# SwiGLU feed-forward on one core: the first 256 rows of x loaded two rows to a partition

## The chip, the core and the metric

The kernel runs on one core of a Trainium2 chip. The metric is device time in microseconds (us) of one execution. The core has a matrix engine (PE, TensorE, with its weight loader shown apart as PEld), VectorE (DVE), ScalarE (ACT), GpSimd (POOL) and SyncE (SP). Transfers between the chip's large memory and the on-chip memory are issued by SP and ACT, each on its own queue; a transfer that has been issued runs beside the engines, on 16 DMA engines. The on-chip memory has 128 partitions. PE writes into PSUM, a second small memory, from which DVE or ACT copy.

## The reference

```python
B, S, D, F = 1, 2048, 640, 1536

def reference(x, w_gate, w_up, w_down):
    g = _silu(x @ w_gate)
    u = x @ w_up
    return (g * u) @ w_down
```

All arrays are bf16. x is 2048 x 640, the gate and up weights 640 x 1536, the down weights 1536 x 640.

## The kernel before

PE contracts over partitions. For the two projections the contraction runs over D = 640, five slices of 128 (`kd`), so x is needed transposed: `xT` has D on the partitions and the 2048 rows along the free dimension. The rows are worked in four blocks of 512. In each block, for each of the 12 slices of F (`fc`), PE makes the gate product `pg` and the up product `pu` (lines 192 to 202, five matmuls each), ACT applies silu, DVE multiplies (lines 211 to 217), and the result goes into `aT`. After the twelve slices the block's down product follows (lines 256 to 308), its results are copied out of PSUM by ACT and stored. DVE also works, beside that, on the last four rows by dot products (line 147).

The transposed x comes in two ways. Rows 256 to 2047 are transposed by the DMA (`turn_x`, line 105, issued by SP). Rows 0 to 255 are needed first, and are loaded as they lie and transposed by PE:

- `load_x` (line 86) brings 128 rows per call into `x_sb`, one row of 640 elements (1280 bytes) to a partition. Rows 0 to 127 are loaded on SP's queue, rows 128 to 255 on ACT's; they are the first instructions of both queues.
- Behind them on SP's queue come, in this order, four of the five early gate-weight pieces (line 115; the piece for `kd` 1 is on ACT's queue), the DMA transpose of rows 256 to 511, the first up-weights in two transfers (line 83), and the rest of the weights.
- `head` first runs 18 matmuls on ones (`warm`, line 176), which need no loaded data. Then `transpose_chunk` (lines 180 to 190) transposes the two chunks of 128 rows. For each chunk there are five transposes, one for each slice of D: the 128 x 128 piece of `x_sb` is loaded as PE's weights and the identity streams through. Slices 0 and 1 go into one PSUM tile and are copied by ACT into `xT`, slices 2 to 4 go into another and are copied by DVE (line 190).
- Then the first projections follow in a fixed order (`steps`, lines 230 to 235): for four slices of F at once, slice `kd` 0 on rows 0 to 127, `kd` 0 on rows 128 to 255, then `kd` 1 to 4 on rows 0 to 255, and then all five on rows 256 to 511. After them come the four up products.

The order of PE's and ACT's instructions in the head is kept as written (`keep_order`); every other wait is one for data or for a free buffer. An SP transfer that uses a semaphore again waits for the earlier transfer on it.

Of the kernel before, what the change touches and what calls it, by code (L numbers as in the profile page):

```python
# [10 lines left out]
def _body(  # L11
# [8 lines left out]
    nc = tc.nc  # L20
    P = nc.NUM_PARTITIONS
    f32 = mybir.dt.float32
    bf16 = mybir.dt.bfloat16
# [3 lines left out]
    B, S0, D = x.shape  # L27
    F = w_gate.shape[1]
    S = B * S0
    x2 = x.rearrange("b s d -> (b s) d")  # L30
# [7 lines left out]
    HALF = S_BLK // 2  # L38
# [10 lines left out]
    consts = ctx.enter_context(tc.tile_pool(name="consts", bufs=1))  # L49
    work = ctx.enter_context(tc.tile_pool(name="work", bufs=3))  # L50
    outp = ctx.enter_context(tc.tile_pool(name="outp", bufs=3))
    psum = ctx.enter_context(
        tc.tile_pool(name="psum", bufs=2, space=bass.MemoryType.PSUM)
    )

    ident = consts.tile([P, P], bf16)
    x_sb = consts.tile([P, HALF // P, D], bf16)
    xT = consts.tile([P, KD, S], bf16)
    wg_sb = consts.tile([P, KD, F], bf16)
    wu_sb = consts.tile([P, KD, F], bf16)  # L60
# [9 lines left out]

    make_identity(nc, ident[:])

    x_v = x2.rearrange("(c p) d -> p c d", p=P)
    xt_v = x2.rearrange("s (kd p) -> s kd p", p=P)
    wg_v = w_gate.rearrange("(kd p) f -> p kd f", p=P)
    wu_v = w_up.rearrange("(kd p) f -> p kd f", p=P)
# [2 lines left out]
    def wslice(a, b):  # L79
        return slice(a * P, b * P)  # L80
# [1 line left out]
    def load_w(eng, dst, src, a, b):  # L82
        eng.dma_start(out=dst[:, :, wslice(a, b)], in_=src[:, :, wslice(a, b)])

    def load_x(eng, c0, c1):
        eng.dma_start(out=x_sb[:, c0:c1, :], in_=x_v[:, c0:c1, :])  # L86

    def issue_order(a, b):
        tc.add_manual_dep(
# [18 lines left out]
    silu_first = consts.tile([P, 1], f32)  # L108
    nc.vector.memset(ones[:], 1.0)  # L109

    load_x(nc.sync, 0, 1)
    load_x(nc.scalar, 1, 2)
    for kd in range(KD):
        eng = nc.scalar if kd == 1 else nc.sync
        eng.dma_start(
            out=wg_sb[:, kd, wslice(0, EARLY)], in_=wg_v[:, kd, wslice(0, EARLY)]
# [12 lines left out]
    def turn_w(dst, src, f0, f1):  # L129
# [7 lines left out]
        out=x_row[:],  # L137
        in_=x2[S - T : S, :].rearrange("t d -> (t d)").partition_broadcast(P),
# [40 lines left out]

    def transpose_chunk(c, parts):  # L180
        c_sl = slice(c * P, (c + 1) * P)
        for copy, tag, k0, k1 in parts:
            pt = psum.tile([P, k1 - k0, P], bf16, tag=tag, name="pt")
            for kd in range(k0, k1):
                nc.tensor.transpose(  # L185
                    out=pt[:, kd - k0, :],
                    in_=x_sb[:, c, kd * P : (kd + 1) * P],
                    identity=ident[:],
                )
            copy(out=xT[:, k0:k1, c_sl], in_=pt[:])  # L190

    def proj_step(ps, w_sb, fc, sb, c0, c1, kd):
        nc.tensor.matmul(  # L193
# [25 lines left out]
    def head():  # L219
        dve, act = nc.vector.tensor_copy, nc.scalar.copy  # L220
        split = [(act, "po_a", 0, 2), (dve, "po_b", 2, KD)]
        pgs = [
            psum.tile([P, S_BLK], f32, tag="gu", name="pg", bufs=4)
            for _ in range(EARLY)
        ]
        warm(N_WARM)
        for c in range(HALF // P):
            transpose_chunk(c, split)

        steps = [(0, 0, P), (0, P, HALF)]  # L230
        steps += [(kd, 0, HALF) for kd in range(1, KD)]
        steps += [(kd, HALF, S_BLK) for kd in range(KD)]
        for kd, c0, c1 in steps:
            for fc in range(EARLY):
                proj_step(pgs[fc], wg_sb, fc, 0, c0, c1, kd)

        for fc in range(EARLY):
            pu = psum.tile([P, S_BLK], f32, tag=("po_a", "po_b")[fc % 2], name="pu")
            proj(pu, wu_sb, fc, 0, 0, S_BLK)
            gate(pgs[fc], pu, 0, fc, S_BLK)  # L240
        keep_order(mybir.EngineType.PE)
        keep_order(mybir.EngineType.Activation)

    head()
    for sb in range(NSB):
# [27 lines left out]
        for q in range(P // Q):  # L273
            nc.scalar.dma_start(
                out=out2[
                    sb * S_BLK : sb * S_BLK + n_t, DA + q * Q : DA + (q + 1) * Q
                ].rearrange("(i r) c -> r i c", r=Q),
                in_=ot_q[q * Q : (q + 1) * Q, :].rearrange("r (i c) -> r i c", c=Q),
            )

        for j in range(SUB):
# [6 lines left out]
            for c0, c1, tag in cols:  # L288
# [14 lines left out]
                eng = nc.sync if c1 < D else nc.scalar  # L303
# [82 lines left out]
def kernel(tc, *args):  # L386
    _body(tc, *args)
    tc.close()
    tc.compile()
    _trim(tc.nc)  # L390
# [30 lines left out]
```

## Time and profile before

| | |
|---|---|
| median of three runs | 163.31 us (163.09 to 163.35) |
| profiled execution, first to last instruction (span) | 161.8 us |
| profiled execution, total | not among the answers; the median stands 1.5 us above the span |
| PE busy | 159.4 us (99%), 808 matmuls |
| PEld busy | 77.6 us (48%), 808 weight loads |
| DVE busy | 111.0 us (69%) |
| ACT busy | 42.6 us (26%) |
| DMA | 15.86 MB, mean 98 GB/s |
| ten transposes of x on PE | from 2.31 us, 1.25 us |
| first projection on PE | 3.71 us |

The profile shows one execution. Its times are microseconds from the first instruction. A row of the timeline gives start, length, engine, line of the kernel, operation, what it writes and reads, and a count; in brackets stands the idle time of that engine before it and what ended it. SPq and ACTq are the two queues' issuing instructions; their length is the issue alone. A row of the DMA view gives the time from issue to landing as its last number. A row of the table by stretches gives the stretch, its length, the busy time and count of PE, PEld, DVE, ACT and POOL, the granted clock, the share of the DMA engines and GB/s; with one line of the kernel asked for, only the engines that this line uses. Matmuls overlap, and the length shown of one (0.31 us for 128 columns) is longer than the distance from one to the next.

### The profile page before, as it was taken

To read this page: it belongs to the slowest core of one execution; us is meant where nothing else is said; L and a number is where in the kernel's file an instruction comes from. 1 tells how busy PE (TensorE), PEld (TensorE's weight loads), DVE (VectorE), ACT (ScalarE), POOL (GpSimd) and SP (SyncE) were. 2 spreads that over 40 slices of the span, in tenths; PEclk is the share of its full clock that TensorE was granted. 3 is DMA by queue.
4 is the path that set the end of the run, shared out by engine and by line. 5 is a ranking of instruction groups with operands and counts; after the bars stand their busy time and mean duration, and the time that the engine had idled before them with its cause. 6 is when DMAs were issued, how large, how long until landed. Compare 5 with 4: busy or idle time off the path is not lost.

```text
span 161.8 us, 2142 instructions
## 1 busy us (share of the span) xinstructions
PE 159.4 (99%) x808; PEld 77.6 (48%) x808; DVE 111.0 (69%) x250; ACT 42.6 (26%) x74; POOL 0.6 (0%) x6
## 2 busy tenths in 40 slices
PE   8999999999999999999999999999999999999995
PEld 7854444444444444444444444444444444445454
DVE  2034223599569999989919999979964999993001
ACT  5051222112222222211222322221214222222121
POOL 1000000000000000000000000000000000000000
PEclk9999999999999999999999999999999999999999
DMA  6999999934189999003110000000321000000312
GB/s 212 231 351 349 361 248 231 222 75 91 34 192 159 235 236 184 4 0 34 65 65 0 0 4 2 0 0 3 62 67 34 0 0 0 0 0 4 48 41 73
DMA packets 41961, 15.86 MB, mean 98 GB/s; under 512 B 33504, under 2 KB 41824, under 8 KB 41952
## 3 DMA queue, kind: packets, MB, share of 16 engines
q1 hardware_dynamic: 33584, 14.93, 37.0%
q10 hardware_dynamic: 8368, 0.80, 3.5%
q8 instruction: 6, 0.10, 0.3%
q14 instruction: 3, 0.02, 0.1%
HBM read 6.88 MB, written 2.62 MB: 59 GB/s over the span
## 4 chain that ended last, share of the span: by engine, by line
PE 97%; DMA 2%; SPq 0%; DVE 0%; issue 0%
PE pg L193 32%; PE pu L193 32%; PE po_a L291 26%; PE po_t L261 6%; DMA wg_sb<-in_w_gate_dram 2%; SPq L86 0%; DVE ot_b L302 0%
## 5 line engine op out<-in xcount | busy, mean ns | idle before, releaser
L193 PE MATMUL pg<-xT,wg_sb 128*128 128x512 bf16 (+3 forms) x264 | 59.8, 363 | 0.1
L193 PE MATMUL pu<-xT,wu_sb 128*128 128x512 bf16 (+1 forms) x240 | 59.1, 379 | 0.0
L215 DVE TENSOR_TENSOR aT<-sg,pu 128x512 bf16<-128x512 f32 (+1 forms) x48 | 32.7, 682 | 32.3 <-PE pu L193 32.3
L214 ACT ACTIVATE sg<-pg 128x512 f32<-128x512 f32 (+1 forms) x48 | 28.4, 597 | 71.2 <-PE pg L193 67.4
L291 PE MATMUL po_a<-wd_sb,aT 128*128 128x512 bf16 (+4 forms) x228 | 42.8, 348 | 0.0
L147 DVE SCALAR_TENSOR_TENSOR prod<-wgT,x_row 128x640 f32<-128x640 bf16 x48 | 39.4, 821 | 1.5 <-DMA wgT<-in_w_gate_dram 0.4
L147 DVE SCALAR_TENSOR_TENSOR prod<-wuT,x_row 128x640 f32<-128x640 bf16 x48 | 39.4, 821 | 1.0
L193 PEld LDWEIGHTS <-wg_sb 128*128 128x128 bf16 x264 | 25.9, 100 | 26.8 <-DMA wg_sb<-in_w_gate_dram 0.4
L193 PEld LDWEIGHTS <-wu_sb 128*128 128x128 bf16 x240 | 23.4, 98 | 28.1 <-DMA wu_sb<-in_w_up_dram 0.3
L291 PEld LDWEIGHTS <-aT 128*128 128x128 bf16 x228 | 20.8, 98 | 21.7
L300 ACT CAST ot<-po_a 128x512 bf16<-128x512 f32 (+2 forms) x17 | 9.5, 559 | 31.8 <-PE po_a L291 20.2
L261 PE MATMUL po_t<-aT,wd_sb 128*128 128x512 bf16 (+1 forms) x48 | 10.4, 366 | 0.0
L261 PEld LDWEIGHTS <-wd_sb 128*128 128x128 bf16 x48 | 4.7, 98 | 5.1
L302 DVE CAST ot_b<-po_a 128x96 bf16<-128x96 f32 (+1 forms) x2 | 0.5, 240 | 9.7 <-PE po_a L291 9.6
L270 ACT CAST ot_t<-po_t 128x512 bf16<-128x512 f32 (+1 forms) x4 | 2.2, 559 | 11.6 <-PE po_t L261 11.6
L147 DVE DVE_READ_ACCUMULATOR prod<-wgT,x_row 128x1 f32 x48 | 3.9, 82 | 0.0
L147 DVE DVE_READ_ACCUMULATOR prod<-wuT,x_row 128x1 f32 x48 | 3.9, 82 | 0.0
L272 DVE STREAM_TRANSPOSE ot_q<-ot_t 128x512 bf16<-128x512 bf16 (+1 forms) x4 | 2.7, 676 | 1.7 <-ACT ot_t L270 1.7
L190 DVE COPY xT<-pt 128x384 bf16<-128x384 bf16 x2 | 0.7, 358 | 2.9 <-PE pt L185 2.9
L176 PE MATMUL pw<-ones 128*128 128x128 bf16 x18 | 2.1, 313 | 0.4 <-DVE ones L109 0.4
L176 PEld LDWEIGHTS <-ones 128*128 128x128 bf16 x18 | 1.8, 147 | 0.4 <-DVE ones L109 0.4
L119 ACT ACT_TABLE_LOAD x1 | 1.3, 1283 | 1.0 <-issue 1.0
(13 smaller groups left out, 4.7 us busy)
## 6 DMA issues: line engine op xcount, KB each, us to landing
wd_sb<-in_w_down_dram SPq DMA_DIRECT2D x1, 1920.0 KB, 13.0
out_dram<-ot SPq DMA_DIRECT2D x15, 128.0 KB, 1.7
wg_sb<-in_w_gate_dram SPq DMA_DIRECT2D x2, 640.0 KB, 7.9
wu_sb<-in_w_up_dram SPq DMA_DIRECT2D x2, 640.0 KB, 8.6
wu_sb<-in_w_up_dram SPq DMA_DIRECT2D x2, 320.0 KB, 4.7
x_row<-in_x_dram SPq DMA_DIRECT2D x1, 640.0 KB, 5.1
wg_sb<-in_w_gate_dram SPq DMA_DIRECT2D x4, 128.0 KB, 3.4
out_dram<-ot_q ACTq DMA_DIRECT2D x12, 32.0 KB, 1.9
```

What stands on the lines that cost most here:

```text
L119: nc.scalar.activation(silu_first[:], ones[:, 0:1], ACT.Silu)
L147: nc.vector.scalar_tensor_tensor(out=prod[:], in0=wT[:, fc, :], scalar=1.0, in1=x_row[:, t, :], op0=ALU.mult, op1=ALU.mult, accum_out=acc[ ...
L176: nc.tensor.matmul(pw[:, 0:P], lhsT=ones[:], rhs=ones[:], start=True, stop=True)
L190: copy(out=xT[:, k0:k1, c_sl], in_=pt[:])
L193: nc.tensor.matmul(ps[:, c0:c1], lhsT=w_sb[:, kd, fc * P : (fc + 1) * P], rhs=xT[:, kd, sb * S_BLK + c0 : sb * S_BLK + c1], start=(kd == 0 ...
L214: nc.scalar.activation(sg[:, 0:n_s], pg[:, 0:n_s], ACT.Silu)
L215: nc.vector.tensor_tensor(out=aT[:, fc, s0 : s0 + n_s], in0=sg[:, 0:n_s], in1=pu[:, 0:n_s], op=ALU.mult)
L261: nc.tensor.matmul(po_t[:], lhsT=wd_sb[:, kf, DA:D], rhs=aT[:, kf, sb * S_BLK : sb * S_BLK + n_t], start=(kf == 0), stop=(kf == KF - 1),)
L270: nc.scalar.copy(ot_t[:], po_t[:])
L272: nc.vector.transpose(out=ot_q[:], in_=ot_t[:])
L291: nc.tensor.matmul(po[:], lhsT=aT[:, kf, s0 : s0 + P], rhs=wd_sb[:, kf, c0:c1], start=(kf == 0), stop=(kf == KF - 1),)
L300: nc.scalar.copy(ot[:], po[:])
```

## The change

Rows 0 to 255 are laid out two to a partition: partition p holds rows 2p and 2p + 1, one behind the other, 2560 bytes that are contiguous in the source. The first load brings rows 0 to 127 into partitions 0 to 63 and the second rows 128 to 255 into partitions 64 to 127, on the same two queues as before. A chunk of 128 rows is then 64 partitions, and each of its five slices is transposed in two steps, one for the even rows and one for the odd rows: the weights are 64 rows by 128 columns, and a 64 x 64 part of the identity streams through. That makes twenty transposes in place of ten. In PSUM the even rows of a slice lie ahead of the odd rows; the copies into `xT` write every second column, so that `xT` is as before. Nothing else is changed.

```diff
-    x_sb = consts.tile([P, HALF // P, D], bf16)
+    H = P // 2
+    x_sb = consts.tile([P, 2, D], bf16)
...
-    x_v = x2.rearrange("(c p) d -> p c d", p=P)
+    x_v = x2[0:HALF, :].rearrange("(p r) d -> p r d", r=2)
...
-    def load_x(eng, c0, c1):
-        eng.dma_start(out=x_sb[:, c0:c1, :], in_=x_v[:, c0:c1, :])
+    def load_x(eng, c):
+        eng.dma_start(out=x_sb[c * H : (c + 1) * H], in_=x_v[c * H : (c + 1) * H])
...
-    load_x(nc.sync, 0, 1)
-    load_x(nc.scalar, 1, 2)
+    load_x(nc.sync, 0)
+    load_x(nc.scalar, 1)
...
     def transpose_chunk(c, parts):
         c_sl = slice(c * P, (c + 1) * P)
+        rows = slice(c * H, (c + 1) * H)
         for copy, tag, k0, k1 in parts:
-            pt = psum.tile([P, k1 - k0, P], bf16, tag=tag, name="pt")
+            pt = psum.tile([P, k1 - k0, 2, H], bf16, tag=tag, name="pt")
             for kd in range(k0, k1):
-                nc.tensor.transpose(
-                    out=pt[:, kd - k0, :],
-                    in_=x_sb[:, c, kd * P : (kd + 1) * P],
-                    identity=ident[:],
-                )
-            copy(out=xT[:, k0:k1, c_sl], in_=pt[:])
+                for r in range(2):
+                    nc.tensor.transpose(
+                        out=pt[:, kd - k0, r, :],
+                        in_=x_sb[rows, r, kd * P : (kd + 1) * P],
+                        identity=ident[rows, rows],
+                    )
+            copy(
+                out=xT[:, k0:k1, c_sl].rearrange("d k (p r) -> d k r p", r=2),
+                in_=pt[:],
+            )
```

## The prediction

> **What bounds the kernel now.** I read the page first: busy times, then the chain that ended last.
>
> ```profile
> span 161.8 us, 2142 instructions
> PE 159.4 (99%) x808; PEld 77.6 (48%) x808; DVE 111.0 (69%) x250; ACT 42.6 (26%) x74; POOL 0.6 (0%) x6
> ...
> PE 97%; DMA 2%; SPq 0%; DVE 0%; issue 0%
> PE pg L193 32%; PE pu L193 32%; PE po_a L291 26%; PE po_t L261 6%; DMA wg_sb<-in_w_gate_dram 2%; SPq L86 0%; DVE ot_b L302 0%
> ```
>
> TensorE (PE) is on the chain for 97% of the span. The only other entry of size is one transfer, a piece of the gate weights, 2% of 161.8 = 3.2 us. The change touches only the first microseconds, so I asked for the chain of the first 16 us and then for the timeline there.
>
> ```profile
> 0.45 3.21 DMA wg_sb<-in_w_gate_dram
> 3.66 0.05 issue
> 3.71 5.21 PE pg L193 x44
> 8.92 4.37 PE pu L193 x20
> ```
>
> ```profile
> 0.00 0.39 SPq L86 DMA_DIRECT2D x_sb<-in_x_dram  x1
> 0.13 0.38 ACTq L86 DMA_DIRECT2D x_sb<-in_x_dram  x1
> ...
> 0.45 1.84 SPq L115 DMA_DIRECT2D wg_sb<-in_w_gate_dram  x4
> ...
> 2.31 0.98 PEld L185 LDWEIGHTS <-x_sb 128*128 128x128 bf16 x10
> 2.31 1.25 PE L185 MATMUL pt<-ident,x_sb 128*128 128x128 bf16 x10
> ...
> 2.33 1.91 SPq L105 DMA_TRANSPOSE xT<-in_x_dram  x1
> 2.74 0.37 ACT L190 COPY xT<-pt 128x256 bf16<-128x256 bf16 x1 [0.22 <-PE pt L185]
> 3.06 0.36 DVE L190 COPY xT<-pt 128x384 bf16<-128x384 bf16 x1 [2.73 <-PE pt L185]
> 3.28 0.37 ACT L190 COPY xT<-pt 128x256 bf16<-128x256 bf16 x1 [0.16 <-PE pt L185]
> 3.60 0.36 DVE L190 COPY xT<-pt 128x384 bf16<-128x384 bf16 x1 [0.17 <-PE pt L185]
> 3.71 4.93 PEld L193 LDWEIGHTS <-wg_sb 128*128 128x128 bf16 x44 [0.41 <-DMA wg_sb<-in_w_gate_dram]
> ...
> 4.29 1.15 SPq L83 DMA_DIRECT2D wu_sb<-in_w_up_dram  x2
> ...
> 8.79 4.00 PEld L193 LDWEIGHTS <-wu_sb 128*128 128x128 bf16 x20 [0.15 <-DMA wu_sb<-in_w_up_dram]
> ```
>
> Read it as a race. The path that the change edits (load x, transpose, copy) has its last weight load done at 2.31 + 0.98 = 3.29, and then the weight loader sits 0.41 us until the first gate-weight piece has landed at 3.66. So the edited path is not the one that releases the projections: it has about 0.3 us to spare (0.41 less one step of 0.10). Behind that stand two more waits, which show as breaks between groups of weight loads, and the landing times of the transfers:
>
> ```profile
> 4.96 1.52 PEld L193 LDWEIGHTS <-wg_sb 128*128 128x128 bf16 x14
> ...
> 6.58 2.06 PEld L193 LDWEIGHTS <-wg_sb 128*128 128x128 bf16 x19
> ```
>
> ```profile
> wu_sb<-in_w_up_dram SPq DMA_DIRECT2D x2, 320.0 KB, 4.7
> ...
> x_sb<-in_x_dram SPq DMA_DIRECT2D x1, 160.0 KB, 2.3
> x_sb<-in_x_dram ACTq DMA_DIRECT2D x1, 160.0 KB, 2.6
> ...
> xT<-in_x_dram SPq DMA_TRANSPOSE x1, 4.2
> ```
>
> From 4.96 a 256-column step takes (1.52 - 0.10)/13 = 0.109 us (0.10 is one load's own length, below). Fourteen of them end at 4.96 + 14 x 0.109 = 6.49, but the next starts at 6.58: 0.09 us lost. There the DMA transpose of rows 256-511 lands (2.33 + 4.2 = 6.53). From 6.58, twenty steps end at 8.76 and the up-weights start at 8.79: 0.03 us lost to their landing. After that PE is dense to the end. So the end time is set, in the last place, by SP's queue: those two transfers are issued at 2.33 and 4.29.
>
> **Pace.** The lengths of single instructions in the edited part and in the projections, and PE's work from 3.71 to 4.96 (the columns after the loads' are granted clock, transfer share and GB/s):
>
> ```profile
> L185 PEld LDWEIGHTS <-x_sb x10: 103/151/151, 2.3 to 3.1; 128*128 128x128 bf16 x10
> L185 PE MATMUL pt<-ident,x_sb x10: 288/314/314, 2.3 to 3.2; 128*128 128x128 bf16 x10
> ```
>
> ```profile
> L193 PEld LDWEIGHTS <-wg_sb x44: 95/98/152, 3.7 to 8.5; 128*128 128x128 bf16 x44
> ```
>
> ```profile
> 3.71:4.96 1.25, 1.25 (x10) 1.13 (x11) 1.00 1.01 264
> ```
>
> A transpose of 128 columns takes (1.25 - 0.31)/9 = 0.104 us. From 3.71 eight projection steps of 128 columns and two of 256, 1536 columns, take 1.25 us: 0.81 ns a column. After 4.96 it is 0.109 us for 256: 0.43. So PE works at half pace until about 4.95, although the clock column reads 1.00 there. A delay of PE before 4.95 therefore costs half of itself, and 0.12 us (0.09 + 0.03) are swallowed by the two later waits.
>
> **The change, part by part.**
>
> *Transposes.* Ten 128-row steps go, twenty 64-row steps with 64 moving columns come, each with its own weight load. No 64-row step is in the trace. The nearest row is the last output tile, 64 columns with a weight load each, at full pace:
>
> ```profile
> 159.46 0.46 PE L291 MATMUL po_a<-wd_sb,aT 128*128 128x64 bf16 x10
> ```
>
> ```profile
> L291 PE MATMUL po_a<-wd_sb,aT 128*128 128x64 bf16 x12 | 0.5, 193 | 0.0
> ```
>
> (0.46 - 0.19)/9 = 0.030 us a step; at half pace 0.06. Twenty take 1.2 us where ten take 1.04: 0.16 us more, inside the 0.3 us to spare. Below, it cannot go under 20 x 0.03 = 0.6 us; above, one step can cost as much as a 128-row step (0.104), or a weight load that does not overlap its matmul (0.15, the load's length in these microseconds, + 0.06 = 0.21). I take 0.06, because the 64-column row keeps its weight loads hidden. At 0.104 the projections start at 2.31 + 20 x 0.104 = 4.39, 0.68 late, worth 0.34 at half pace, less 0.12: +0.22 us. At 0.21 they start at 6.5, when 1.24 us of half-pace work (0.62) and 1.52 us of full-pace work stand undone: 2.14 - 0.12 = +2.0 us.
>
> The Trainium skill, "TensorE: Matmul & The Clock Gate", Part 3, "The mechanism", says that a weight load overlaps a running matmul only when it goes to another row group; here all ten steps of a half go to the same one. By that the step would be the 0.21 us above. The trace of the full-height steps disagrees (ten loads of 0.15 fit in 0.98 us beside their matmuls), so I keep it as a rival only.
>
> *PSUM copies.* Same four instructions, same elements, writing every second column. Nearest above: the copies at 0.36 to 0.37; far above, 512 elements on VectorE:
>
> ```profile
> L215 DVE TENSOR_TENSOR aT<-sg,pu 128x512 bf16<-128x512 f32 (+1 forms) x48 | 32.7, 682 | 32.3 <-PE pu L193 32.3
> ```
>
> So VectorE's copy of 384 is between 0.36 and 0.68, ScalarE's between 0.37 and 0.68; below nothing can be gained, since neither ends a wait. I take 0.55 and 0.37. The cover: the second VectorE copy would end at 3.06 + 2 x 0.55 = 4.2, or 4.4 at 0.68, and its columns (third of five contraction slices) are first read after 8 steps of 128 columns and 8 of 256 from 3.71, past 5. Zero. ScalarE's second copy ends at 3.65 and is read after four steps, at 4.1; zero as long as the second load lands less than 0.45 later. Without that cover each copy would cost its increase at half pace, under 0.2 us.
>
> *The two loads.* The same 160 KB each on the same queues; 64 rows of 2560 bytes in place of 128 of 1280, into half of the partitions each. Behind the first, on SP, stand four gate pieces, the DMA transpose and the up-weights; behind the second, on ACT, one gate piece. The issue takes 0.39 us; I leave it at that (with half the rows it could be less, at best 0.39 less for all that follows on SP; the 0.46 a piece of the next four on the queue shows no such saving). How the transfers share the engines:
>
> ```profile
> 1.00:2.30 1.30, 1.30 (x14) 1.23 (x12) 0.00 (x0) 1.28 (x1) 0.00 (x0) 1.00 0.94 275
> 2.30:3.40 1.10, 1.10 (x12) 0.98 (x10) 0.34 (x1) 0.70 (x4) 0.00 (x0) 1.00 0.93 312
> 3.40:3.70 0.30, 0.16 (x2) 0.00 (x0) 0.12 (x2) 0.25 (x1) 0.00 (x0) 1.00 0.67 184
> ...
> 5.80:7.10 1.30, 1.30 (x13) 1.09 (x12) 0.00 (x0) 0.00 (x0) 0.00 (x0) 1.00 0.56 141
> 7.10:8.75 1.65, 1.65 (x17) 1.37 (x15) 0.00 (x0) 0.12 (x1) 0.00 (x0) 1.00 1.06 323
> ```
>
> The last column is GB/s. The engines are full from the first packets until 3.4, so what x takes longer, the weights land later. 328 KB of x at 275 GB/s are 1.19 us. Lower end: at 323 GB/s 1.02, -0.17 us. Upper end: a load into half of the partitions runs at half of the rate and the two follow one another, 328 KB at 312/2 = 156 GB/s, 2.10 us, +0.91. I take +0.1, near the row of the same bytes on the same two queues: the two loads are issued 0.13 us apart, so for that long one is alone with half of the partitions. The thin stretch at 3.40 to 3.70 (184 in place of 312 GB/s) can take up 0.3 x (1 - 184/312) = 0.12 of it. The next thin one, 5.80 to 7.10, is empty because SP issues late, so the up-weights do not move with the stream.
>
> What a late stream costs: the DMA transpose is the first to tell. It delays PE at 6.58 one for one, less 0.03.
>
> *Sum.* Transposes 0 (covered), copies 0 (covered), issue 0, loads between 0 and 0.07: I put +0.05. The answers give the profiled execution's span, 161.8 us, and no total for it; 163.31, the median of the runs, stands 1.5 us above, which I hold fixed. 163.31 + 0.05 = 163.36, rounded 163.4. A measurement of this kernel tells about 0.2%, 0.33 us, from no change (the three runs before spread over 0.26).
>
> **The rivals.**
>
> *The half-height loads are slow (slower).* Place: the transfer queues from 1.0 to 3.4 us. Price: between +0.5 and +0.91 us of stream; less 0.12 and 0.03, 163.7 to 164.1. It decides from 0.48 us of added transfer time (0.33 + 0.15). For: the stream is full there, and each load now fills 64 partitions. Against: both are in flight together and fill all 128. The Trainium skill, "SBUF — State Buffer", sections "Door 1: The DMA port swizzle (why [64,N] ≈ [32,N])" and "Can I just issue two DMAs to hit both halves?", speaks against the change: partitions 0-63 reach 8 of 16 ports, 196 GB/s, and a load at 0 with one at 64 was only 6% faster than one alone. By it, an estimate, 328 KB at 208 GB/s are 1.58 us, +0.39, and 163.31 + 0.39 - 0.15 = 163.55. No row of this trace shows a 64-partition load.
>
> *The 64-row steps are slow (slower).* Above 0.115 us a step the loss passes 0.33: the start is then 4.61, 0.9 late, 0.45 at half pace, less 0.12. At 0.21 a step, 165.3; halfway, at 0.16, the start is 5.5, 0.62 + 0.55 - 0.12 = 1.05 and 164.4. For: twice as many weight loads, all in one half of the rows. Against: the 64-column row above.
>
> *PE reaches full pace later (slower).* Each microsecond costs half: 0.7 us decide, one gives 163.8, three 164.8. For: the pace changes 4.5 us after PE begins, and what it counts is not shown; half-height steps may count less. Against: the columns that stream stay the same.
>
> *The pieces land sooner (faster).* If larger rows help, PE starts at 2.31 + 1.2 = 3.5 at best in place of 3.71, worth 0.1 at half pace, and the two waits give 0.12: 163.31 - 0.22 = 163.1. That is still inside 0.2%, so a real gain would need an earlier full pace too (0.22 us sooner for the missing 0.11), near 162.9.
>
> **How the numbers follow.** Hidden, no change: 0.48, at 163.4, own range 163.1 to 163.6 (from the two waits and the earlier start, -0.22, to steps of 0.104, +0.22, with the loads' +0.05). Slow loads 0.26, slow steps 0.11, late pace 0.05: slower 0.42. Faster past 0.33: 0.10. The range reaches down to 163.0 (half of the faster case out) and up to 164.4 (most of the slow loads and half of the slow steps in): about 0.13 is left out.
>
> **What would show it.** Right: twenty transposes about 0.06 apart, the last one started before 3.6; the wait on the gate piece still there, 0.2 to 0.35 long; full pace from about 4.95; the up-weights' first matmul at 8.8 to 8.9. Wrong: x landing past 2.9 with the DMA transpose past 6.8 (slow loads); steps over 0.11 apart and no wait on the gate piece (slow steps); 256-column steps at 0.21 after 5.5 (late pace).

## The result and the profile after

| | before | changed |
|---|---|---|
| median | 163.49 us (163.09 to 163.88, 6 runs) | 187.24 us (186.43 to 188.45, 6 runs) |
| ratio to before | | 1.1443, 95% interval 1.1404 to 1.1482 |
| span of the profiled execution | 161.8 us | 185.1 us |
| first projection on PE | 3.71 us | 26.35 us |

The changed kernel is 14% slower. The loss isn't spread: it is one wait at the start. The page of the changed kernel shows it as a hole, in its head, its row of PE over 40 slices, and the chain that ended last:

```profile
span 185.1 us, 2153 instructions
...
PE 159.7 (86%) x806; PEld 78.2 (42%) x818; DVE 111.4 (60%) x250; ACT 42.6 (23%) x74; POOL 0.6 (0%) x6
...
PE   7000039999999999999999999999999999999995
...
PE 84%; DMA 7%; SPq 6%; issue 1%; ACT 0%; DVE 0%; ACTq 0%
PE pg L199 29%; PE pu L199 28%; PE po_a L297 23%; DMA xT<-in_x_dram 7%; PE po_t L267 5%; SPq L84 3%; SPq L126 1%; SPq L116 1%; SPq L106 1%; SPq L87 0%; ACT xT L193 0%; DVE ot_b L308 0%; ACTq L193 0%
```

PE is busy as long as before (159.7 against 159.4 us), but does nothing in slices two to five and in most of the sixth (a slice is 4.6 us). A transfer into `xT`, 7% of the span, stands on the chain in place of the gate weights. The chain of the first 35 us, in order of time, and the view of waits of the first 30 us (engine, line, what it waited for, total, times, longest):

```profile
2.66 1.55 SPq L106
...
12.53 13.24 DMA xT<-in_x_dram
25.77 0.02 issue
25.79 0.02 ACTq L193
25.81 0.04 issue
25.86 0.45 ACT xT L193
26.31 0.04 issue
26.35 5.89 PE pg L199 x44
```

```profile
DVE xT L193 <- DMA xT<-in_x_dram: 25.5, 1, 25.5
ACT xT L193 <- DMA xT<-in_x_dram: 22.9, 1, 22.9
PE pg L199 <- ACT xT L193: 21.9, 1, 21.9
```

Both copy engines (line 193) hold their first copy until the second DMA transpose into `xT` has landed. That transpose (rows 512 to 1023) is issued at 12.53, behind all weights on SP's queue, and lands 13.24 us later. The timeline of the head shows that what the copies needed had long been there:

```profile
0.00 0.57 SPq L87 DMA_DIRECT2D x_sb<-in_x_dram  x1
0.13 0.56 ACTq L87 DMA_DIRECT2D x_sb<-in_x_dram  x1
...
3.00 1.25 PEld L188 LDWEIGHTS <-x_sb 64*128 64x128 bf16 x20 [0.77 <-DMA x_sb<-in_x_dram]
3.00 1.41 PE L188 MATMUL pt<-ident,x_sb 64*128 64x64 bf16 x20 [0.51 <-DMA x_sb<-in_x_dram]
...
25.86 0.75 ACT L193 COPY xT<-pt 128x256 bf16<-128x256 bf16 x2 [22.86 <-DMA xT<-in_x_dram]
25.87 1.05 DVE L193 COPY xT<-pt 128x384 bf16<-128x384 bf16 x2 [25.54 <-DMA xT<-in_x_dram]
26.35 3.92 PE L199 MATMUL pg<-xT,wg_sb 128*128 128x128 bf16 x26 [21.94 <-ACT xT L193]
```

The twenty transposes are over at 4.4. The copies write columns 0 to 255 of `xT`, the DMA transposes columns 256 to 1023; no element is written by both. The program itself, as built, holds the wait. The first copies on ACT in both kernels, with what they wait for (DMAHW7 is the semaphore that the first two DMA transposes into `xT` share):

```
before   L190 TensorCopy xT<-pt 128x2x128   [waits PE]           x2
changed  L193 TensorCopy xT<-pt 128x2x2x64  [waits DMAHW7, PE]
         L193 TensorCopy xT<-pt 128x2x2x64  [waits PE]
```

So the layer that records the kernel and places the semaphores took the copies' write, once it went in steps of two columns, to overlap with the transfers recorded ahead of it. How it compares two patterns isn't shown here. The sum closes: the first projection is 26.35 - 3.71 = 22.64 us later, and the 44 gate matmuls of the head take 5.89 in place of 5.21 us, 0.68 more, because PE works at half pace for 2.9 us after the hole, where it did for 1.25 us from the same point before. 22.64 + 0.68 = 23.3, which is 185.1 - 161.8.

### The profile page after: what moved, and what is told of

Read it like the earlier page. It is cut to its first block, busy times and chain, and to the rows that moved or that the text cites. A ratio compares the mean times of both kernels' runs of the same rounds, so it can differ in the third digit from the quotient of the medians.

```text
span 185.1 us, 2153 instructions
## 1 busy us (share of the span) xinstructions
PE 159.7 (86%) x806; PEld 78.2 (42%) x818; DVE 111.4 (60%) x250; ACT 42.6 (23%) x74; POOL 0.6 (0%) x6
## 4 chain that ended last, share of the span: by engine, by line
PE 84%; DMA 7%; SPq 6%; issue 1%; ACT 0%; DVE 0%; ACTq 0%
PE pg L199 29%; PE pu L199 28%; PE po_a L297 23%; DMA xT<-in_x_dram 7%; PE po_t L267 5%; SPq L84 3%; SPq L126 1%; SPq L116 1%; SPq L106 1%; SPq L87 0%; ACT xT L193 0%; DVE ot_b L308 0%; ACTq L193 0%
## 5 line engine op out<-in xcount | busy, mean ns | idle before, releaser
L193 ACT COPY xT<-pt 128x256 bf16<-128x256 bf16 x2 | 0.8, 446 | 22.9 <-DMA xT<-in_x_dram 22.9
```

The costliest lines, as they stand in the source:

```text
L193: copy(out=xT[:, k0:k1, c_sl].rearrange("d k (p r) -> d k r p", r=2), in_=pt[:],)
```

## The experiments

Theory A is the wait just told. Theory B is that the chip is slow at what is new (half-height loads, 64-row steps, stepped copies) and that the wait is only where it shows.

**plain_write**: the changed kernel, with the step moved from the write to the read.

```diff
             copy(
-                out=xT[:, k0:k1, c_sl].rearrange("d k (p r) -> d k r p", r=2),
-                in_=pt[:],
+                out=xT[:, k0:k1, c_sl],
+                in_=pt[:].rearrange("d k r p -> d k p r"),
             )
```

> The changed kernel, its loads and its twenty transposes kept, but the copies write the plain 128 columns and it is the PSUM side that is read with a step. Same result. Theory A (the copies were made to wait for both DMA transposes into xT because their write had a step of two): no wait on xT before the copies, first projection at about 4.34 us as the gate piece lands, second wait at about 7.1 as the DMA transpose lands (2.66 + 4.4), 0.5 us above the kernel before: 164.0 (163.7 to 164.4). Theory B (the chip is slow at the half-height loads, the 64-row steps or stepped copies, and the wait is a symptom): stays above 180.

Measured: 164.67 us, ratio 1.0064 (1.0043 to 1.0085), 0.3 above the range of theory A and far from theory B. 22.6 of the 23.8 us are gone by turning one access pattern over. The copies follow the transposes at once, as the timeline of this kernel shows:

```profile
2.94 1.34 PE L188 MATMUL pt<-ident,x_sb 64*128 64x64 bf16 x20 [0.44 <-DMA x_sb<-in_x_dram]
3.36 0.37 ACT L193 COPY xT<-pt 128x256 bf16<-128x256 bf16 x1 [0.36 <-PE pt L188]
3.68 1.19 DVE L193 COPY xT<-pt 128x384 bf16<-128x384 bf16 x2 [3.35 <-PE pt L188]
...
4.20 6.05 PE L199 MATMUL pg<-xT,wg_sb 128*128 128x128 bf16 x44
```

**stepped_view_in_before**: the kernel before, with nothing changed but the way in which the copy is written.

```diff
-            copy(out=xT[:, k0:k1, c_sl], in_=pt[:])
+            copy(
+                out=xT[:, k0:k1, c_sl].rearrange("d k (p r) -> d k r p", r=2),
+                in_=pt[:].rearrange("d k (p r) -> d k r p", r=2),
+            )
```

> The kernel before, its loads and its ten transposes kept, with only the copies written as even columns and then odd columns, on both sides, so that each column goes where it went. Theory A: the copies wait for the second DMA transpose as in the changed kernel, which is issued at about 12 and lands at about 25.5 us: first projection near 26, about 23 us above the kernel before, 186 to 187. Theory B: nothing but the copies' length moves, 163.5.

Measured: 187.2 us, ratio 1.1435 (1.1394 to 1.1476), the whole loss of the change without its loads and without its transposes. The chain of its first 40 us:

```profile
12.05 13.53 DMA xT<-in_x_dram
25.58 0.02 issue
25.61 0.02 ACTq L190
25.62 0.04 issue
25.67 0.45 ACT xT L190
26.12 0.04 issue
26.16 7.29 PE pg L196 x44
```

**later_transpose**: the changed kernel, with the second DMA transpose recorded after the copies.

```diff
-    turn_x(S_BLK, 2 * S_BLK)
-    nc.sync.dma_start(out=x_row[:], ...)
-    turn_w(wgT, wgt_v, 0, KF - WT_STEP)
...
     head()
+    turn_x(S_BLK, 2 * S_BLK)
+    nc.sync.dma_start(out=x_row[:], ...)
+    turn_w(wgT, wgt_v, 0, KF - WT_STEP)
```

> The changed kernel with the second DMA transpose (rows 512 to 1023) and what follows it on SP recorded after the head in the program, in the same place of SP's queue. Theory A: the copies now wait for the first DMA transpose only, landing at about 7.1; first projection at 7.6 in place of 26.35, about 3.9 us above the kernel before plus up to 0.8 for a later full pace: 167.4 to 168.3. Theory B: no change, 187.

Measured: 169.0 us, ratio 1.0323 (1.0289 to 1.0358). The wait moved to the transpose that is still recorded ahead, as A says; SP's queue is in the same order. The chain of its first 14 us:

```profile
2.66 4.80 DMA xT<-in_x_dram
...
7.54 0.45 ACT xT L187
8.00 0.04 issue
8.04 6.03 PE pg L193 x34
```

The price was 0.7 above the top of its range, and the last row says where: 34 matmuls fill 6.03 us (the view ends there), where before 44 took 5.21. PE ran at half pace until about 13.3, 5.3 us after the hole: up to there a 256-column step takes 0.213 us, after it 0.109.

With these three, theory B is out for the 14%. What it names is left with the 0.6% of plain_write. The next kernels ask about that.

**full_height_loads**: plain_write, with each load bringing one row of all 128 partitions.

```diff
-        eng.dma_start(out=x_sb[c * H : (c + 1) * H], in_=x_v[c * H : (c + 1) * H])
+        eng.dma_start(out=x_sb[:, c], in_=x_v[:, c])
```

> The kernel of plain_write with the two loads cut the other way: each brings one of the two rows of all 128 partitions, 1280 bytes to a partition; the twenty transposes are kept. If the loads into 64 partitions are what lands late (3.0 and 3.5 after issue in the changed kernel, 2.3 and 2.6 before), both land as before, at about 2.3 and 2.75, the transposes start at 2.75 because the first chunk needs both loads, the gate piece lands near 3.7 again, and the time is within 0.2 of the kernel before: 163.6. If the lateness has another cause, x lands past 3 again and the time is that of plain_write, 164.0.

Measured: 165.22 us, ratio 1.0086 (1.0056 to 1.0115). The first half of the expectation held: issues back to 0.40 us, landings 2.5 and 2.8 after issue, in place of 0.57 and 2.9 and 3.4. The time didn't follow: 165.22 is above both of the times expected. The timeline, and the landing lines of the view of `x_sb` (least, median, most) here and then of plain_write:

```profile
0.00 0.40 SPq L87 DMA_DIRECT2D x_sb<-in_x_dram  x1
0.12 0.40 ACTq L87 DMA_DIRECT2D x_sb<-in_x_dram  x1
...
3.90 6.08 PE L199 MATMUL pg<-xT,wg_sb 128*128 128x128 bf16 x44
```

```profile
DMA to landing us min/median/max: 2.5/2.7/2.8
```

```profile
DMA to landing us min/median/max: 2.9/3.1/3.4
```

In this execution, the fastest of the four, the projections start 0.3 us earlier than in plain_write, but take 6.08 us, as there. What is left in it is mostly the pace, not the landing.

**one_load**: plain_write, with all of x in one load on SP.

```diff
-        eng.dma_start(out=x_sb[c * H : (c + 1) * H], in_=x_v[c * H : (c + 1) * H])
+        eng.dma_start(out=x_sb[:], in_=x_v)
...
     load_x(nc.sync, 0)
-    load_x(nc.scalar, 1)
```

> The kernel of plain_write with one load on SP for all 256 rows, two rows (2560 bytes) to each of 128 partitions; ACT's queue starts with its gate piece. If the half of the partitions makes the loads late, this issue is back at 0.40 us and all of x lands by about 2.7; if the 2560-byte pieces do, the issue stays at 0.57 and x lands past 3.0. Time: with x at 2.7, PE idle 0.4, full pace near 7 as in full_height_loads, 164.5 to 165.2.

Measured: 164.35 us, ratio 1.0053 (1.0031 to 1.0075). The timeline and the landing line:

```profile
0.00 0.40 SPq L87 DMA_DIRECT2D x_sb<-in_x_dram  x1
...
4.15 6.01 PE L198 MATMUL pg<-xT,wg_sb 128*128 128x128 bf16 x44
```

```profile
DMA to landing us min/median/max: 3.1/3.1/3.1
```

Pieces of 2560 bytes are issued in 0.40 us when they go to 128 partitions and in 0.57 when they go to 64, so the longer issue belongs to the 64 partitions. The landing was missed: 3.1, not 2.7, for twice the bytes in one load; the time is 0.15 below the range expected.

**plain_write_warm24**: plain_write with `N_WARM = 24`, so that PE is not idle while x comes (theory C), against theory D, that half-height steps count less towards full pace.

```diff
-    N_WARM = 18
+    N_WARM = 24
```

> The kernel of plain_write with 24 matmuls on ones in place of 18, so that PE has work from 0.39 to about 2.93, when x lands there. Theory C (PE reaches full pace later, at 7.26 in place of 4.95, because it sat idle 0.65 us waiting for x): full pace comes near 5 again, worth (7.26 - 5)/2 = 1.1 us, 163.6 (163.3 to 163.9). Theory D (full pace comes later because the twenty transposes are half as high and count less): pace and time stay, 164.7.

Measured: 164.05 us, ratio 1.0037 (1.0009 to 1.0064), with single runs from 163.46 to 165.44. The first eight projection steps, in this kernel and then in plain_write:

```profile
4.13 0.56 PEld L199 LDWEIGHTS <-wg_sb 128*128 128x128 bf16 x8
```

```profile
4.20 0.77 PEld L199 LDWEIGHTS <-wg_sb 128*128 128x128 bf16 x8
```

In the profiled execution PE was at full pace already there: most of these steps start 0.056 us apart, where it is 0.107 in plain_write. But it then waited for a gate piece, and again for the DMA transpose of rows 256 to 511, which landed at 2.66 + 4.5 = 7.16:

```profile
5.12 4.39 PE L199 MATMUL pg<-xT,wg_sb 128*128 128x256 bf16 x36 [0.25 <-DMA wg_sb<-in_w_gate_dram]
...
7.17 2.06 PEld L199 LDWEIGHTS <-wg_sb 128*128 128x128 bf16 x19 [0.30 <-issue]
```

So an early pace is given back at the landings. The median stands 0.6 us below that of plain_write, half of what was expected, and the intervals of the two ratios overlap: the fall isn't clear of the noise.

**before_warm12**: the kernel before with `N_WARM = 12`, which puts an idle time in.

> The kernel before with 12 matmuls on ones in place of 18: PE is idle from about 1.65 to 2.31, as long as in plain_write, and everything else is as it was. Theory C: full pace comes at about 7.1 in place of 4.95, 1.1 us less the 0.12 of the two later waits: 1.0 above the kernel before, 164.6. Theory D: nothing changes, 163.6.

Measured: 164.04 us, ratio 1.0028 (1.0005 to 1.0050). The sign is C's, the size is 0.4 us in place of 1.0. The profiled execution bears the mechanism out in sign alone: PE idled 0.69 us, and full pace came at 5.5, later than 4.95 but not at 7.1. Then PE waited for the DMA transpose, which landed 4.8 us after issue in place of 4.2:

```profile
7.17 2.34 PE L193 MATMUL pg<-xT,wg_sb 128*128 128x256 bf16 x20 [0.29 <-DMA xT<-in_x_dram]
```

**half_height_warm**: the kernel before with its matmuls on ones over 64 rows.

```diff
-                pw[:, 0:P], lhsT=ones[:], rhs=ones[:], start=True, stop=True
+                pw[:, 0:P], lhsT=ones[0:64], rhs=ones[0:64], start=True, stop=True
```

> The kernel before with its 18 matmuls on ones contracting over 64 rows in place of 128; same columns, same length, no idle time added; the value is thrown away in both. Theory D (half-height steps count less towards full pace): full pace comes one to two us later, 164.2 to 164.7. Theory C: 163.6.

Measured: 163.92 us, ratio 1.0009 (0.9988 to 1.0030). No loss that can be told from none, although the profiled execution, at 163.99 us, had its 44 gate matmuls slow:

```profile
3.66 6.18 PE L193 MATMUL pg<-xT,wg_sb 128*128 128x128 bf16 x44
```

So one profile doesn't price the pace: it differs between executions of one kernel. D isn't borne out; up to 0.3% of it stays possible. Half-height transposes with the loads of before weren't tried.

**before_warm21**: the kernel before with `N_WARM = 21`, in search of a better head.

> The kernel before with 21 matmuls on ones in place of 18, PE busy until about 2.6. In profiles of kernels with the old loads x landed between 2.27 and 2.60, so PE idles up to 0.3 us before the transposes in some executions. If idle time there delays full pace (theory C), the median falls by 0.1 to 0.4, 163.3; if the time of full pace is only the phase of something that runs by itself, it stays within 0.1, and where x lands early the three matmuls cost up to 0.1.

Measured: 163.61 us, ratio 0.9995 (0.9978 to 1.0012). No gain, although full pace came at 4.3 in the profiled execution: PE then waited until 6.69 for the DMA transpose, so in this execution the wait and not the pace ended last, as in that of plain_write_warm24:

```profile
6.69 2.34 PE L193 MATMUL pg<-xT,wg_sb 128*128 128x256 bf16 x20 [0.36 <-DMA xT<-in_x_dram]
```

No kernel that ran was shown to be faster than the kernel before.

**plain_write_again**: plain_write once more.

> The kernel of plain_write once more, to size what is left of the change without the wait: 164.6, ratio 1.005 to 1.008. Its profile tells whether x lands late again (2.9 and 3.5) and whether full pace comes at 7.3 again or at another time; if at another time with the same median, one profile doesn't price it.

Measured: 165.13 us, ratio 1.0071 (1.0046 to 1.0096). x landed at 2.8 and 3.5 after issue, late again; the projections began at 4.31 and full pace came at 8.3, a microsecond later than in the first plain_write. The median is 0.5 above the 164.6 expected, the ratio within what was expected.

## Why the prediction was wrong

The prediction was 163.4 us within 163.0 to 164.4, with 0.42 for slower; measured were 187.24. No rival held the cause.

- **The step that failed** is the one on the PSUM copies: "Same four instructions, same elements", "Zero". It priced their length and named the work that covers it. It didn't ask what else they wait for. Line 190 writes `xT`, and two DMA transposes write the same tile earlier in the program; whether the copies must wait for them is decided by how the write's pattern is compared with theirs. The plain write was told apart, the stepped one wasn't. The 22.9 us that ACT's first copy waits for the transfer stand in the sum at nothing. stepped_view_in_before shows that this alone costs 14%. The sentence on the kernel before, that every other wait is one for data or for a free buffer, no longer holds in the changed kernel.
- Copies, length: VectorE's was put at 0.55, measured 0.58 with the stepped write and 0.56 with the stepped read; ScalarE's at 0.37, measured 0.45 and 0.37. So VectorE's was right and ScalarE's 0.08 short, inside its bounds; neither is a part of the loss. In the cover that goes with them, four steps of 256 columns stand ahead of the third slice, not eight; "past 5" holds all the same, at about 5.2.
- Transposes: 0.06 a step. In plain_write twenty take 1.34 us with a wait for the second load inside; (1.34 - 0.24)/19 = 0.058, 0.24 being the length of one; in plain_write_again ten of their weight loads, 0.10 to 0.13 us long each, fit in 0.56 us, about 0.05 a step. Right. The rival of slow steps (0.115 and above) is out. The Trainium skill, "TensorE: Matmul & The Clock Gate", Part 3, "The mechanism", says that a weight load overlaps a running matmul only when it goes to another row group; this case's trace disagrees, since ten loads in a row into the same 64 rows ran beside their matmuls at that distance.
- The two loads: +0.1 us, with a rival at +0.5 to +0.91. In the changed kernel they landed 3.0 and 3.5 after issue, against 2.3 and 2.6; other kernels with the old loads had 2.5 to 2.9. That is 0.4 to 0.9 late, so the size taken was too small and the rival's was about right. Of the rival's two signs, x past 2.9 came; the DMA transpose past 6.8 came too, but it tells nothing, because it landed anywhere from 6.5 to 7.2 in kernels with the old loads. The sentence "The issue takes 0.39 us; I leave it at that" was wrong by 0.18.

```profile
x_sb<-in_x_dram SPq DMA_DIRECT2D x1, 160.0 KB, 3.0
x_sb<-in_x_dram ACTq DMA_DIRECT2D x1, 160.0 KB, 3.5
```

- From the Trainium skill, "SBUF — State Buffer", sections "Door 1: The DMA port swizzle (why [64,N] ≈ [32,N])" and "Can I just issue two DMAs to hit both halves?", the prediction worked out an estimate of +0.39 us of transfer time for the two half-height loads. The runs: plain_write's second load landed 0.13 + 3.4 = 3.5, full_height_loads' 0.12 + 2.8 = 2.9. The direction agrees, 0.6 us, of which 0.17 is the issue. Pieces of 2560 bytes into all partitions (one_load) landed at 3.1, in between. The traces tell the landing; that ports are the reason isn't shown.
- The 0.3 us to spare ahead of the projections: used up in plain_write (start at 4.20 in place of 3.71). The rest of its loss is the pace: 6.05 against 5.21 us for 44 matmuls. 0.49 + 0.84 = 1.33 of the 1.5 us between the spans; the rest isn't placed.
- "PE reaches full pace later" had 0.05 and was priced at half of the delay. The sum held full pace at 4.95 whatever the change does. In the nine profiled executions without the long wait it came anywhere from 3.8 to 8.3 (there the distance from one step to the next halves): at 3.8 to 5.0 in the three where PE had no idle time ahead of the transposes, at 5.5 to 8.3 in the six where it had 0.1 to 0.7 us. That speaks for idle time as a part of it, but its length doesn't order them, and each is one execution. How the 0.6% divides between late landing and late pace is not settled.

## What to carry to other kernels

When a copy's write gets a step, ask which other instructions write the same tile, and read the waits of the built program before pricing it: a wait placed for safety can cost far more than the instruction. Not every stepped write need draw one; here the copies of two and three slices of a tile with DMA transposes into its other columns did. If there is a choice, put the step on the read of a private tile and keep the write to a shared tile plain. And a wait on a transfer lasts until the queue has come to that transfer and it has landed, here 25.8 us into the kernel.

## What the runs showed that was not expected

- A load of 160 KB into 64 partitions took 0.57 us to issue on SP and 0.54 to 0.56 on ACT; into 128 partitions 0.40, with twice the bytes too.
- After a hole PE starts at half pace, and full pace comes at no fixed time. After the hole of 22 us the half pace lasted 2.9 us in one kernel and 5.7 in another; their 44 gate matmuls took 5.89 and 7.29 us. Ahead of the hole PE had not been at full pace either: in the changed kernel the 64-row steps started 0.053 us apart, and 0.029 apart in the second ten of plain_write_warm24.
- Matmuls on ones that fill PE's idle time in the head bought little: twenty-one in place of eighteen gained nothing in the kernel before, and in plain_write twenty-four gained at most half of what the profile of one execution had promised. Where full pace came early, PE waited at the DMA transpose instead.
